# Weights from float64: the lower word's shift made by ScalarE as a scaled, rounded integer

## The chip, the cores and the metric

One NeuronCore of a Trainium2 chip runs the whole program. The metric is device time in microseconds (us) from start to end of one execution. Beside its tensor engine (TensorE; PE and, for weight loads, PEld in the profile) the core has VectorE (DVE), ScalarE (ACT), GpSimd (POOL) and SyncE (SP), which here issues all DMA transfers.

## What is computed

A chunked state-space scan ("attention") on x (4 x 8 x 768 x 32), followed by two dense expert layers on the 3072 tokens with 256 features:

```python
y = scan(x, a, B, C)                  # chunks of 32 tokens, state 16 x 32 per head
x = y as (3072, 256)
h = x @ moe_w_in;  g = maximum(0.01 * h, h);  x = g @ moe_w_out      # 256 -> 2048 -> 256
h = maximum(x @ moe2_w_in, 0);  out = (h * h) @ moe2_w_out           # 256 -> 2048 -> 256
```

The inputs of the scan are float32; the four weight matrices (524,288 numbers each) are float64 and enter the core as pairs of 32-bit words.

## The kernel before

**Scan.** 12 pieces (4 batches, 3 pieces of 256 tokens each). `scan_piece` is a generator of 24 small steps: scale factors (`mx`, `sc`), the decay scans `lt` and `e1`, fp16 halves of the operands, block-diagonal copies (`kbd`, `xbh`, `xbl`, `sbd`), three sets of small matmuls (`S`, then `Y` twice), the state scan `stt`, and at the end `yh` (line 334, ScalarE) and `yl` (line 335, VectorE), one pair for each of the two feature halves: the input of the experts as a rounded part and a rest.

**Experts.** Every product is made of three matmuls (high x low, high x high, low x high). `Phase.hmm` (lines 363 to 365) makes 512 columns of the hidden layer, `act` takes them from PSUM on ScalarE and splits them into `gh` and `gl` (line 379, VectorE; in layer 2 also the square of line 377), `omm` (lines 391 to 396) makes the output. `ORDER` names the phases (layer, block of pieces); `due` says how many scan steps are to be done at which place.

**Weights.** The four matrices are cut into 8 pieces each, `[128, 2, 256]` 64-bit words, 512 KB. A piece goes through four functions, and one call of `w_step` moves four pieces on by one function each:

- `load_w` (line 118): the transfer into the tile `wst`;
- `split_w` (line 127, ScalarE): the upper words `w1`, taken as f32, are scaled by 2^-112;
- `split_w1` (VectorE): line 133 shifts the lower words `w0` right by 29 bits, so that the three bits stay that end an f32 mantissa; line 134 puts in the upper word shifted left by 3, line 135 the sign: `w0` is the f32 value;
- `split_w2`: line 146 (ScalarE) rounds it to the matmul's format, line 147 (VectorE) makes the rest.

`w0` and `w1` are every second word of the tile, a stride of 8 bytes. Eight calls of `w_step` follow the first piece of the scan, others are called between the groups of the experts' first phases.

**Order.** When the program is built, a scheduler orders the instructions of each engine by what is ready; an engine then runs its queue in that order, each instruction behind its waits. So a change of one operation's engine can change the order of everything around it.

Of the kernel before, what the change touches and what calls it, by code (L numbers as in the profile page):

```python
# [10 lines left out]
F16 = mybir.dt.float16  # L11
I32 = mybir.dt.int32
I64 = mybir.dt.int64
AF = mybir.ActivationFunctionType
ALU = mybir.AluOpType
AX = mybir.AxisListType
# [26 lines left out]
def ssd_moe_kernel(ctx: ExitStack, tc: tile.TileContext, in1, in2, w1i, w1o, w2i, w2o, out):  # L43
# [6 lines left out]
    nc = tc.nc  # L50
# [17 lines left out]
    lr = cp.tile([4, P], F32, name="lr")  # L68
    nc.scalar.activation(lr, ones, AF.Lrelu)
    delta = cp.tile([P, U, T], F16, name="delta")  # L70
# [37 lines left out]
    def load_w():  # L108
        nm, c = wq.pop(0)
        if nm == "2o" and c >= 5:  # L110
            st = yp.tile([P, 2, 256], I64, tag="y2", name="wst")
        else:
            st = wp.tile([P, 2, 256], I64, tag="w", name="wst")
        if nm[1] == "i":
# [6 lines left out]
    def split_w():  # L121
        nm, c, sl, st = w_loaded.pop(0)
        v = st.bitcast(I32).rearrange("p k (f two) -> p k f two", two=2)
        w0, w1 = v[:, :, :, 0], v[:, :, :, 1]


        nc.scalar.activation(w1.bitcast(F32), w1.bitcast(F32), AF.Copy, scale=2.0**-112)
        w_half.append((nm, c, sl, w0, w1))

    def split_w1():  # L130

        nm, c, sl, w0, w1 = w_half.pop(0)
        nc.vector.tensor_single_scalar(w0, w0, 29, ALU.logical_shift_right)  # L133
        nc.vector.scalar_tensor_tensor(w0, w1, 3, w0, ALU.logical_shift_left, ALU.bitwise_or)  # L134
        nc.vector.scalar_tensor_tensor(w0, w1, -(1 << 31), w0, ALU.bitwise_and, ALU.bitwise_or)  # L135
        w_full.append((nm, c, sl, w0.bitcast(F32)))

    def split_w2():
# [5 lines left out]
        else:  # L144
            h, l = w_hi[nm][sl], w_lo[nm][sl]
        nc.scalar.activation(h, w, AF.Copy)
        nc.vector.tensor_tensor(l, w, h.bitcast(F32), ALU.subtract)  # L147

    def w_step():
        if w_full:  # L150
            split_w2()
        if w_half:
            split_w1()
        if w_loaded:
            split_w()
        if wq:
            load_w()
# [15 lines left out]
    def scan_piece(p, tiles, get_y):  # L173
# [59 lines left out]
        ch = sp.tile([P, U, T], F16, tag="f2", name="ch")  # L233
        nc.scalar.activation(him, bt_t, AF.Copy, scale=sbp)
        nc.scalar.activation(ch, ct_t, AF.Copy, scale=scc)
        yield
# [16 lines left out]
        xh = sp.tile([P, U, D], F16, tag="xh", name="xh")  # L253
        nc.scalar.activation(xh, x_t, AF.Copy, scale=sx)
        yield
# [298 lines left out]
```

## Time and profile before

| | |
|---|---|
| time, median of 3 runs (lowest to highest) | 662.59 us (661.88 to 662.81) |
| the profiled execution: its time; its span | 663.11 us; 661.3 us |
| busy: PE, DVE, ACT | 605.9, 466.9, 400.6 us |
| mean granted TensorE clock | 0.984 of full speed |
| chain that ended last | PE 72%, DVE 19%, ACT 5% |

The span goes from the first to the last instruction; the execution's time is 1.8 us longer. An engine's busy time is the time in which it ran anything. A mean duration of one instruction includes its latency; two that follow each other without a wait overlap, so their common time is less than the sum. In the strips of 40 slices a digit is the busy share in tenths.

### The profile page before, as it was taken

To read this page: it belongs to the slowest core of one execution; us is meant where nothing else is said; L and a number is where in the kernel's file an instruction comes from. 1 tells how busy PE (TensorE), PEld (TensorE's weight loads), DVE (VectorE), ACT (ScalarE), POOL (GpSimd) and SP (SyncE) were. 2 spreads that over 40 slices of the span, in tenths; PEclk is the share of its full clock that TensorE was granted. 3 is DMA by queue.
4 is the path that set the end of the run, shared out by engine and by line. 5 is a ranking of instruction groups with operands and counts; after the bars stand their busy time and mean duration, and the time that the engine had idled before them with its cause. 6 is when DMAs were issued, how large, how long until landed. Compare 5 with 4: busy or idle time off the path is not lost.

```text
span 661.3 us, 11324 instructions
## 1 busy us (share of the span) xinstructions
PE 605.9 (92%) x4464; PEld 521.1 (79%) x4464; DVE 466.9 (71%) x1016; ACT 400.6 (61%) x714; POOL 5.2 (1%) x14
## 2 busy tenths in 40 slices
PE   0286679998989999999999999999999999999997
PEld 0285679998889888899988788778788878788886
DVE  7989998999998884398594497583596422554543
ACT  4877686866678584395484485475575443444442
POOL 3000000000000000000000000000000000000000
PEclk9997789999999999999999999999999999999999
DMA  8663434110122020010020020030000000000000
GB/s 324 237 186 123 149 96 129 41 65 10 41 73 73 1 89 1 1 64 26 1 88 1 0 73 1 1 104 0 1 1 1 1 32 2 0 1 0 33 1 32
DMA packets 12469, 34.80 MB, mean 53 GB/s; under 512 B 1152, under 2 KB 2176, under 8 KB 12416
## 3 DMA queue, kind: packets, MB, share of 16 engines
q1 hardware_dynamic: 12416, 34.08, 15.8%
q8 instruction: 35, 0.57, 0.4%
q14 instruction: 18, 0.15, 0.1%
HBM read 30.93 MB, written 3.15 MB: 52 GB/s over the span
## 4 chain that ended last, share of the span: by engine, by line
PE 72%; DVE 19%; ACT 5%; issue 2%; DMA 2%; SPq 0%; DVEq 0%; ACTq 0%
PE o L391 12%; PE hp L363 11%; PE hp L364 11%; PE o L392 11%; PE hp L365 11%; PE o L396 11%; DVE gl L379 3%; DVE wst L135 2%; DVE wst L134 2%; DMA wst<-w1i 1%; DVE wst L133 1%; DMA wst<-w2i 1%; DVE e L260 1%; DVE lt L244 1%; DVE w2o L147 1%
## 5 line engine op out<-in xcount | busy, mean ns | idle before, releaser
L379 DVE TENSOR_TENSOR gl<-t,gh 128x512 fp32r<-128x512 f32 x192 | 132.0, 688 | 124.8 <-ACT t L374 81.8
L373 ACT ACTIVATE gh<-hp 128x512 fp32r<-128x512 f32 x96 | 57.3, 597 | 85.8 <-PE o L392 69.4
L378 ACT CAST gh<-t 128x512 fp32r<-128x512 f32 x96 | 59.5, 620 | 59.8 <-DVE t L377 47.1
L391 PE MATMUL o<-gh,wl1o 128*128 128x256 f32 (+1 forms) x256 | 89.0, 361 | 3.4 <-DVE wl1o L147 3.4
L363 PE MATMUL hp<-yl,wh1i 128*128 128x256 f32 (+1 forms) x256 | 88.9, 348 | 3.1 <-DVE yl L335 1.7
L364 PE MATMUL hp<-yh,wh1i 128*128 128x256 f32 (+1 forms) x256 | 88.8, 347 | 0.0
L365 PE MATMUL hp<-yh,wl1i 128*128 128x256 f32 (+1 forms) x256 | 88.1, 344 | 0.0
L377 DVE TENSOR_TENSOR t<-t 128x512 f32<-128x512 f32 x96 | 66.1, 689 | 30.3 <-ACT t L376 29.9
L391 PE MATMUL o<-gh,w2o 128*128 128x256 f32 (+1 forms) x256 | 84.3, 345 | 3.3 <-DVE yl L404 1.4
L363 PE MATMUL hp<-yl,wh2i 128*128 128x256 f32 (+1 forms) x256 | 86.8, 339 | 0.0
L365 PE MATMUL hp<-yh,wl2i 128*128 128x256 f32 (+1 forms) x256 | 86.6, 338 | 0.0
L364 PE MATMUL hp<-yh,wh2i 128*128 128x256 f32 (+1 forms) x256 | 86.3, 337 | 0.0
L392 PE MATMUL o<-gh,wh1o 128*128 128x256 f32 (+1 forms) x256 | 85.6, 348 | 0.0
L376 ACT ACTIVATE t<-hp 128x512 f32<-128x512 f32 x96 | 57.4, 598 | 45.8 <-PE hp L365 44.0
L392 PE MATMUL o<-gh,w2o 128*128 128x256 f32 (+1 forms) x256 | 82.0, 336 | 0.0
L396 PE MATMUL o<-gl,wh1o 128*128 128x256 f32 (+1 forms) x256 | 63.4, 349 | 0.9 <-DVE gl L379 0.9
L396 PE MATMUL o<-gl,w2o 128*128 128x256 f32 (+1 forms) x256 | 61.6, 339 | 0.0
L391 PEld LDWEIGHTS o<-gh,wl1o 128*128 128x128 f32 x256 | 50.4, 197 | 12.3 <-DVE wl1o L147 4.0
L363 PEld LDWEIGHTS hp<-yl,wh1i 128*128 128x128 f32 x256 | 50.0, 196 | 9.4 <-DVE yl L335 2.1
L374 ACT ACTIVATE t<-hp 128x512 f32<-128x512 f32 x96 | 56.9, 593 | 0.0
L391 PEld LDWEIGHTS o<-gh,w2o 128*128 128x128 f32 x256 | 48.1, 188 | 10.9 <-DVE yl L404 2.1
L364 PEld LDWEIGHTS hp<-yh,wh1i 128*128 128x128 f32 x256 | 50.1, 196 | 6.3 <-issue 0.9
(148 smaller groups left out, 1101.9 us busy)
## 6 DMA issues: line engine op xcount, KB each, us to landing
in<-in SPq DMA_DIRECT2D x12, 640.0 KB, 3.9
in<-in SPq DMA_DIRECT2D x12, 512.0 KB, 3.5
wst<-w1i SPq DMA_DIRECT2D x8, 512.0 KB, 8.6
wst<-w1o SPq DMA_DIRECT2D x8, 512.0 KB, 4.0
wst<-w2o SPq DMA_DIRECT2D x8, 512.0 KB, 3.5
wst<-w2i SPq DMA_DIRECT2D x8, 512.0 KB, 4.0
out_t<-ob SPq DMA_DIRECT2D x8, 256.0 KB, 2.3
out_t<-ob SPq DMA_DIRECT2D x8, 128.0 KB, 2.5
```

The lines of the kernel that those rows point to most:

```text
L363: nc.tensor.matmul(hp, wh, self.xl[:, k, :n], start=(k == 0), stop=False)
L364: nc.tensor.matmul(hp, wh, self.xh[:, k, :n], start=False, stop=False)
L365: nc.tensor.matmul(hp, wl, self.xh[:, k, :n], start=False, stop=(k == KI - 1))
L373: nc.scalar.activation(gh, hp, AF.Lrelu)
L374: nc.scalar.activation(t, hp, AF.Lrelu)
L376: nc.scalar.activation(t, hp, AF.Relu)
L377: nc.vector.tensor_tensor(t, t, t, ALU.mult)
L378: nc.scalar.copy(gh, t)
L379: nc.vector.tensor_tensor(gl, t, gh.bitcast(F32), ALU.subtract)
L391: nc.tensor.matmul(self.o[d], wl, gh, start=(m == 0), stop=False)
L392: nc.tensor.matmul(self.o[d], wh, gh, start=False, stop=False)
L396: nc.tensor.matmul(self.o[d], wh, gl, start=False, stop=(m == KO - 1))
```

## The change

The shift of line 133 is taken out of `split_w1`. In its place `split_w` issues a second ScalarE instruction: it reads `w0` as an unsigned 32-bit integer, multiplies it by a little less than 2^-29, adds a little less than -0.5, and writes the result rounded to an integer, which is the word's upper three bits.

```diff
     def split_w():
         ...
         nc.scalar.activation(w1.bitcast(F32), w1.bitcast(F32), AF.Copy, scale=2.0**-112)
+
+
+        nc.scalar.activation(
+            w0, w0.bitcast(U32), AF.Copy, scale=2.0**-29 * (1 - 2.0**-14), bias=7.5 * 2.0**-14 - 0.5
+        )
         w_half.append((nm, c, sl, w0, w1))

     def split_w1():

         nm, c, sl, w0, w1 = w_half.pop(0)
-        nc.vector.tensor_single_scalar(w0, w0, 29, ALU.logical_shift_right)
         nc.vector.scalar_tensor_tensor(w0, w1, 3, w0, ALU.logical_shift_left, ALU.bitwise_or)
         nc.vector.scalar_tensor_tensor(w0, w1, -(1 << 31), w0, ALU.bitwise_and, ALU.bitwise_or)
```

In the changed file line 127 becomes 128, the new instruction is line 131, lines 134 and 135 become 139 and 140, and every later line is 5 higher (146, 147, 334 and 335 become 151, 152, 339 and 340).

The order changes on all engines until about the fourth piece of the scan. Three places:

VectorE, first piece of the scan, where the scale factors `sc` are made between the first two weight pieces. Before:

```order
L135 SCALAR_TENSOR_TENSOR wst<-wst 128x512
L195 TENSOR_SCALAR dg<-ident,m_134 3x3
L133 TENSOR_SCALAR wst<-wst 128x512
L203 TENSOR_SCALAR eb<-S 128x3
L134 SCALAR_TENSOR_TENSOR wst<-wst 128x512
L204 TENSOR_SCALAR eb<-eb 128x3
L147 TENSOR_TENSOR wl1i<-wst,wh1i 128x2x256
L205 TENSOR_SCALAR sc<-eb 128x3
L206 TENSOR_SCALAR isc<-eb 128x3
L244 SCALAR_TENSOR_TENSOR lt<-in_117,delta 128x512
```

And after:

```order
L140 SCALAR_TENSOR_TENSOR wst<-wst 128x512
L200 TENSOR_SCALAR dg<-ident,m_134 3x3
L139 SCALAR_TENSOR_TENSOR wst<-wst 128x512
L208 TENSOR_SCALAR eb<-S 128x3
L152 TENSOR_TENSOR wl1i<-wst,wh1i 128x2x256
L209 TENSOR_SCALAR eb<-eb 128x3
L249 SCALAR_TENSOR_TENSOR lt<-in_117,delta 128x512
L210 TENSOR_SCALAR sc<-eb 128x3
```

The scan `lt` now stands ahead of `sc`; it stood behind it.

ScalarE, first piece, from the copy of the state's input (`d1s`) to the first `yh`. Before:

```order
L306 ACTIVATE d1s<-Y,kk 128x32x8
L314 CAST shl<-stt 128x16x16
L127 ACTIVATE wst<-wst 128x512
L146 ACTIVATE wh1i<-wst 128x2x256 x2
L127 ACTIVATE wst<-wst 128x512
L180 COPY sbd<-t_305 32x16x32 x2
L127 ACTIVATE wst<-wst 128x512
L334 ACTIVATE yh<-Y,fac 128x256
```

And after:

```order
L311 ACTIVATE d1s<-Y,kk 128x32x8
L128 ACTIVATE wst<-wst 128x512
L131 ACTIVATE wst<-wst 128x512
L319 CAST shl<-stt 128x16x16
L151 ACTIVATE wh1i<-wst 128x2x256 x2
L128 ACTIVATE wst<-wst 128x512
L131 ACTIVATE wst<-wst 128x512
L185 COPY sbd<-t_305 32x16x32 x2
L128 ACTIVATE wst<-wst 128x512
L131 ACTIVATE wst<-wst 128x512
L128 ACTIVATE wst<-wst 128x512
L339 ACTIVATE yh<-Y,fac 128x256
```

Two splits stand between `d1s` and `shl`, where there was none, and three instead of one between `sbd` and `yh`.

ScalarE, second piece of the scan, ahead of its `kbd` copies. Before:

```order
L146 ACTIVATE wh1o<-wst 128x512
L374 ACTIVATE t<-hp 128x512
L127 ACTIVATE wst<-wst 128x512 x2
L373 ACTIVATE gh<-hp 128x512
L235 ACTIVATE ch<-in_298,sc 128x512
L234 ACTIVATE him<-in_299,sbp 128x512
L254 ACTIVATE xh<-in_298,sc 128x512
```

And after:

```order
L379 ACTIVATE t<-hp 128x512
L128 ACTIVATE wst<-wst 128x512
L131 ACTIVATE wst<-wst 128x512
L128 ACTIVATE wst<-wst 128x512
L151 ACTIVATE wh1o<-wst 128x512
L240 ACTIVATE ch<-in_298,sc 128x512
L239 ACTIVATE him<-in_299,sbp 128x512
L259 ACTIVATE xh<-in_298,sc 128x512
L378 ACTIVATE gh<-hp 128x512
```

Three splits stand there instead of two, and an expert group's `gh` has moved behind the scan's three operations.

## Rows read from the trace of the kernel before

**Rows 1.** The page: busy time of the engines, and their share in 40 slices.

```profile
PE 605.9 (92%) x4464; PEld 521.1 (79%) x4464; DVE 466.9 (71%) x1016; ACT 400.6 (61%) x714; POOL 5.2 (1%) x14
...
PE   0286679998989999999999999999999999999997
...
DVE  7989998999998884398594497583596422554543
ACT  4877686866678584395484485475575443444442
...
PEclk9997789999999999999999999999999999999999
```

**Rows 2.** Busy time of each engine by stage (us from the span's start).

```profile
core 0: us, PE busy (x) PEld busy (x) DVE busy (x) ACT busy (x) POOL busy (x), PEclk, DMA share, GB/s
...
8.00:33.80 25.80, 4.85 (x114) 4.48 (x114) 24.73 (x62) 20.96 (x36) 0.00 (x0) 1.00 0.80 286
33.80:79.10 45.30, 33.19 (x288) 30.59 (x289) 42.43 (x97) 32.82 (x59) 0.00 (x0) 0.87 0.47 149
79.10:115.40 36.30, 32.47 (x325) 31.33 (x324) 33.23 (x82) 26.39 (x48) 0.00 (x0) 0.88 0.38 119
115.40:168.30 52.90, 49.59 (x484) 47.44 (x484) 52.27 (x115) 38.19 (x69) 0.00 (x0) 1.00 0.14 44
168.30:270.00 101.70, 97.93 (x911) 87.69 (x912) 80.64 (x199) 68.91 (x127) 0.00 (x0) 1.00 0.13 42
270.00:661.30 391.30, 387.31 (x2347) 319.48 (x2345) 229.25 (x458) 211.73 (x375) 0.00 (x0) 1.00 0.06 20
```

**Rows 3.** Groups by line and shape: busy us, mean ns | idle before.

```profile
L133 DVE TENSOR_SCALAR wst<-wst 128x512 int32<-128x512 int32 x32 | 13.2, 420 | 1.2 <-DMA wst<-w1i 1.1
...
L180 ACT COPY xbh<-xh 32x512 f16<-32x512 f16 x48 | 29.4, 613 | 0.6
L127 ACT ACTIVATE wst<-wst 128x512 f32<-128x512 f32 x32 | 21.7, 686 | 11.9 <-DMA wst<-w1i 6.4 <-DMA wst<-w2i 4.3 <-DMA wst<-w1o 0.6
...
L254 ACT ACTIVATE xh<-in,sc 128x512 f16<-128x512 f32 x12 | 8.6, 716 | 0.0
```

**Rows 4.** Timeline, pairs back to back: start us, us of both, engine, line.

```profile
23.56 1.26 ACT L127 ACTIVATE wst<-wst 128x512 f32<-128x512 f32 x2
...
30.80 0.76 DVE L133 TENSOR_SCALAR wst<-wst 128x512 int32<-128x512 int32 x2
31.48 1.29 DVE L134 SCALAR_TENSOR_TENSOR wst<-wst 128x512 int32<-128x512 int32 x2
```

**Rows 5.** VectorE's waits from 8 to 170 us: total us, times, longest.

```profile
DVE wl1i L147 <- ACT wh1i L146: 2.1, 2, 1.8
DVE mkl L292 <- ACT mkh L283: 1.6, 1, 1.6
```

**Rows 6.** Timeline of TensorE: matmuls after its largest gaps [idle before <-releaser].

```profile
33.81 0.58 PE L363 MATMUL hp<-yl,wh1i 128*128 128x256 f32 x1 [1.71 <-DVE yl L335]
...
58.16 0.21 PE L275 MATMUL S<-ch,kbd 128*128 128x32 f16 x1 [4.28 <-ACT kbd L180]
...
73.51 0.39 PE L391 MATMUL o<-gh,wl1o 128*128 128x256 f32 x1 [2.92 <-DVE wl1o L147]
...
95.43 0.18 PE L275 MATMUL S<-ch,kbd 128*128 128x32 f16 x1 [3.41 <-DVE kbd L180]
```

**Rows 7.** Timeline of VectorE: first `yl` of pieces two, three and four.

```profile
79.07 0.48 DVE L335 SCALAR_TENSOR_TENSOR yl<-Y,fac,yh 128x256 fp32r<-128x256 f32 x1
...
115.38 0.47 DVE L335 SCALAR_TENSOR_TENSOR yl<-Y,fac,yh 128x256 fp32r<-128x256 f32 x1
...
168.32 0.48 DVE L335 SCALAR_TENSOR_TENSOR yl<-Y,fac,yh 128x256 fp32r<-128x256 f32 x1
```

**Rows 8.** Timeline of ScalarE in stage A: two of its waits.

```profile
12.63 0.72 ACT L235 ACTIVATE ch<-in,sc 128x512 f16<-128x512 f32 x1 [1.11 <-DVE sc L205]
...
32.15 0.47 ACT L334 ACTIVATE yh<-Y,fac 128x256 fp32r<-128x256 f32 x1 [0.42 <-PE Y L327]
```

More of the change, by code (lines that the diff above doesn't have):

```diff
@@ L13 @@
 I64 = mybir.dt.int64
+U32 = mybir.dt.uint32
 AF = mybir.ActivationFunctionType
```

## The prediction

> **What bounds the kernel now.** I read the page first, then the table by stages, then the waits, then the order of the two engines that the change touches. On the page TensorE is busy for 92% of the span, so over the whole program it sets the time [rows 1]. But its slices are low at the left edge and uneven up to about a quarter of the span, while VectorE shows 9 in eight of its first eleven slices. The average hides two regimes, so I cut the span where each of the first four scan pieces hands its `yl` to TensorE: the first matmul of the experts comes at 33.81 us [rows 6], and the next three pieces' first `yl` subtractions start at 79.07, 115.38 and 168.32 us [rows 7].
>
> The table by these stages [rows 2] shows: from 8 us to the first expert matmul (stage A) VectorE is busy 24.73 of 25.8 us; in stage B (33.8 to 79.1) 42.43 of 45.3; in C (to 115.4) 33.23 of 36.3; in D (to 168.3) 52.27 of 52.9. After that it falls to 80.64 of 101.7 and then to 229.25 of 391.3. ScalarE is busy 20.96, 32.82, 26.39 and 38.19 us in A to D: loaded, but not full. TensorE's idle time is 45.3 - 33.19 = 12.1 us in B, 3.8 in C, 3.3 in D, 3.8 in the next 102 us and 4.0 in all of the rest. VectorE itself waits little before 170 us; its longest waits there add up to 2.1 and 1.6 us, both for ScalarE [rows 5]. So until about 168 us VectorE is the engine that hands out the work; then TensorE is full, and nothing on the other engines matters.
>
> Can VectorE's relief reach the end? Only where TensorE waits. Its four large gaps [rows 6] are 1.71 us at 33.81 (for `yl`, VectorE), 4.28 us at 58.16 (for `kbd`, ScalarE), 2.92 us at 73.51 (for `wl1o`, VectorE) and 3.41 us at 95.43 (for `kbd`, VectorE). What can be won at most is the idle time of B, C and D, 19.2 us, plus what a faster start gives. All 32 shifts stand ahead of the fourth piece's `yl`; later nothing changes but the moment at which the rest begins.
>
> **What one operation costs.** The removed shift takes 420 ns, 32 times [rows 3]; back to back two take 0.76 us, so one more costs VectorE 0.34 us [rows 4]. 32 x 0.34 = 10.9 us leave VectorE. The two operations that stay on VectorE cost 0.60 us each back to back (1.29 us for two) [rows 4]. The added ACTIVATE has no row of its own. Its nearest is line 127, the same engine, the same tile with the same 8-byte stride, 128x512 words in and out: 686 ns, or 0.57 us back to back (1.26 us for two) [rows 3, 4]. A copy from fp16 to fp16 takes 613 ns and one from f32 to fp16 with a scale read from a tile 716 ns [rows 3], so word types and a scalar operand move it by a tenth. I take 0.57 us (ends 0.54 and 0.64): 32 x 0.57 = 18.2 us more on ScalarE. So each word moved costs more than it frees: 0.57 against 0.34.
>
> The Trainium skill has a rule against this (ScalarE: Activation LUTs, Rules for kernel authors): multiplies and adds belong on VectorE, which is faster per element. The rows agree on the price, 420 against 686 ns; by the engine time alone the sum would be 18.2 - 10.9 = 7.3 us longer, 669.9 us.
>
> **What moves.** The instructions of each engine are not laid down in program order, and the two printed orders differ in all of A to D, not by one swap per weight piece. I count what stands ahead of each piece's first `yl` on VectorE and first `yh` on ScalarE.
>
> Stage A. VectorE loses 6 shifts (2.0 us), but the new order puts one more line-134, two more line-135 and one more line-147 operation ahead of the first `yl` (2.4 us): net +0.4. ScalarE gets nine more splits and one more rounding, less one line 127: +9 x 0.57 = 5.1 us ahead of the first `yh`, and it has 25.8 - 20.96 = 4.8 us free. In the two places shown, `sc` now stands behind the scan `lt` (so `ch`, which already waits 1.11 us for `sc` [rows 8], starts about 1.1 us later), and two more splits stand ahead of `yh` (1.1 us against a wait of 0.42 us there [rows 8]: about 0.7 more). The ends are 0 and +5.1; I take **+1.3**, a little under 1.8, since some slack lies between.
>
> Stage B. On VectorE ten shifts go and two line-135 operations have already been done in A: -10 x 0.34 - 2 x 0.60 = -4.6 us. ScalarE gets 11 more: +6.3, which makes 39.1 of 45.3 us against VectorE's 37.8. The two engines hand work to each other all the time, and now neither has much air. Ends 0 and -4.6; I take about half, **-2.2**.
>
> Stage C. Five shifts go (-1.7), two weight operations are already done (-1.2), and two reductions of the next piece come ahead of the mark (+1.2 at the same 0.60): -1.7 us. ScalarE +10 x 0.57 = 5.7: 32.1 of 36.3, VectorE 31.5. Ends 0 and -1.7; I take **-1.2**, more than half, as the two engines are even and TensorE's largest gap here waits for VectorE [rows 6].
>
> Stage D. Eleven shifts go (-3.7); the two reductions were done in C, and one `wl`, two `gl` and one square fall behind the mark (six operations, -3.6): -7.3 us. ScalarE gets almost nothing here (two splits, one rounding less and one relu less). But TensorE is idle only 3.3 us, and part of that is its wait for other things. Ends 0 and -3.3; I take **-1.5**.
>
> SyncE's queue gets a few loads in a different place, among them one weight load ahead of the second piece's second input, which is needed only in stage B; the waits of line 127 for its data are hidden as soon as ScalarE is later than before, so I cost both at nothing. GpSimd's order is unchanged. After D TensorE's order is the same in both kernels except for a few rows.
>
> Sum: +1.3 - 2.2 - 1.2 - 1.5 = -3.6 us. The profiled execution took 663.11 us, so 659.5; the median of the runs, 662.59, is 0.5 lower, so **659.0 us**.
>
> **Rivals.** *ScalarE takes over as the bound (slower).* Its queue is in order, and the scan's copies (`kbd`, `mkh`, `d1s`, `shl`, `sbd`, `yh`) now stand behind the added splits. For it: 39.1 us against 37.8 in B, 32.1 against 31.5 in C, and the largest gap of TensorE already waits for ScalarE's `kbd` [rows 6]. Against it: in D ScalarE has 52.9 - 38.19 = 14.7 us of air. It decides as soon as ScalarE's work ahead of a piece's `kbd` or `yh` ends later than VectorE's. Price: the whole +5.1 in A, nothing won in B and C, -1.5 in D: +3.6, 666.2 us. The rule of the skill above points here.
>
> *VectorE's relief comes through whole.* A at 0, B -4.6, C -1.7, D -3.3: -9.6, 653.0 us. On top, the clock: in B and C its mean is 0.87 and 0.88 of full speed, in A and D 1.00 [rows 2]. With two levels, 2.4 and 1.2 GHz, that is 2 x (0.13 x 45.3 + 0.12 x 36.3) = 20.5 us at the lower level, up to 10.2 us of matmul time lost; the three largest gaps lie in these same two stages [rows 6]. If the gaps shrink and a third of this goes, 3.4 us more are won: 649.6 us. For it: VectorE is nearly without waits up to 170 us. Against it: ScalarE's load, and the largest gap waits for ScalarE. The skill (TensorE: Matmul & The Clock Gate, HAM oscillation) describes waits that put the clock back in just this way; the low clock in these stages agrees.
>
> *No change.* The order puts other weight work where the shifts were, as in A, and TensorE's idle time in B to D stays: within 1.3 us of 662.6.
>
> *The edit does not do what it says.* If an integer in and out took the engine two passes, the new operation would cost some 0.57 us more, 6.3 us in B and 5.1 in A on an engine without that air: about +8 on top, 671 us. The even times of fp16 and f32 copies [rows 3] speak against it.
>
> **How the numbers follow.** Forecast 0.45, ScalarE as the bound 0.25, whole relief 0.15, no change 0.12, a dearer operation 0.03. A difference of 0.2%, 1.3 us, is what a measurement of this kernel can tell from none. Faster: 0.45 + 0.15 = 0.60; same 0.12; slower 0.25 + 0.03 = 0.28. The range goes from 651.5, inside the whole relief without the clock, to 666.5, just past ScalarE as the bound; outside lie the clock's part of the one, some of the other and the dear operation. The forecast's own range, with the ends of A to D half used, is 655 to 661.
>
> **What would show it.** Right: the new line on ScalarE at 0.65 to 0.72 us, VectorE's total down by some 13 us, ScalarE's up by 22; the first expert matmul 0.5 to 2 us later than 33.81; the second piece's `yl` earlier than 79.07 by about 1 us, the fourth's earlier than 168.32 by 3 to 6; TensorE's busy time the same, and its idle time in B to D under 16 us. Wrong: the second `yl` later than 80 us with ScalarE above 90% busy in B (the first rival), or a fourth `yl` 8 us earlier with an end that follows it.

## The result and the profile after

The changed kernel takes 653.71 us (median of 4 runs, 653.03 to 654.31) against 662.24 us of the kernel before (660.41 to 662.81): a ratio of 0.9876, 95% interval 0.9852 to 0.9899, so 8.2 us faster by the ratio. The forecast was 659.0 us, 3.6 us faster; nearest to the measured time is the rival "VectorE's relief comes through whole", put at 653.0. Of all executions of this document one, of 1182.74 us in the run e11 below, lies some 500 us outside the rest of its kernel and is in none of the figures.

The profiled execution took 654.30 us with a span of 652.5 us, 8.8 us less than the 661.3 before. The marks and stages of the kernel before come from an execution of 663.11 us, 0.9 above the median, so a difference of single executions may be off by about as much. The page's busy times and granted clock (against [rows 1]):

```profile
PE 601.4 (92%) x4464; PEld 517.9 (79%) x4464; DVE 456.5 (70%) x984; ACT 415.9 (64%) x746; POOL 5.1 (1%) x14
...
PEclk9997889999999999999999999999999999999999
```

VectorE lost 10.4 us and 32 instructions, ScalarE gained 15.3 us and 32. TensorE's busy time fell by 4.5 us with the same 4464 matmuls; its idle time (span less busy time) fell from 55.4 to 51.1 us. So about half of the 8.8 us is idle time of TensorE, and half is time that it no longer took for the same matmuls.

The same stages as in [rows 2], cut at this kernel's own marks (first expert matmul, first `yl` of pieces two to four):

```profile
core 0: us, PE busy (x) PEld busy (x) DVE busy (x) ACT busy (x) POOL busy (x), PEclk, DMA share, GB/s
8.00:35.38 27.38, 4.85 (x114) 4.48 (x114) 24.91 (x58) 25.36 (x45) 0.00 (x0) 1.00 0.82 281
35.38:75.14 39.76, 31.83 (x296) 29.56 (x296) 38.04 (x85) 38.71 (x71) 0.00 (x0) 0.89 0.54 175
75.14:108.91 33.77, 30.76 (x317) 29.55 (x317) 31.33 (x77) 31.23 (x59) 0.00 (x0) 0.93 0.37 115
108.91:155.05 46.14, 43.74 (x447) 42.73 (x447) 45.18 (x98) 34.50 (x65) 0.00 (x0) 1.00 0.12 39
```

In A and B VectorE and ScalarE are both busy for 91 to 97% of the time; in C for 93 and 92%. Two engines that hand each other work were both that full here, which the forecast did not believe. The marks themselves, from the timelines of TensorE and VectorE (against [rows 6] and [rows 7]):

```profile
35.38 0.58 PE L368 MATMUL hp<-yl,wh1i 128*128 128x256 f32 x1 [1.68 <-DVE yl L340]
...
75.14 0.48 DVE L340 SCALAR_TENSOR_TENSOR yl<-Y,fac,yh 128x256 fp32r<-128x256 f32 x1
...
108.91 0.48 DVE L340 SCALAR_TENSOR_TENSOR yl<-Y,fac,yh 128x256 fp32r<-128x256 f32 x1
...
155.05 0.48 DVE L340 SCALAR_TENSOR_TENSOR yl<-Y,fac,yh 128x256 fp32r<-128x256 f32 x1
...
187.24 0.48 DVE L340 SCALAR_TENSOR_TENSOR yl<-Y,fac,yh 128x256 fp32r<-128x256 f32 x1 [1.50 <-ACT yh L339]
```

The fifth piece's `yl` in the kernel before, not shown yet:

```profile
196.52 0.48 DVE L335 SCALAR_TENSOR_TENSOR yl<-Y,fac,yh 128x256 fp32r<-128x256 f32 x1 [0.52 <-ACT yh L334]
```

Beside them, what the prediction counted of VectorE's own work ahead of each mark (its terms for VectorE, added up from the start):

| mark | before, us | after, us | moved | VectorE's count |
|---|---|---|---|---|
| first expert matmul | 33.81 | 35.38 | +1.6 | +0.4 |
| second `yl` | 79.07 | 75.14 | -3.9 | -4.2 |
| third `yl` | 115.38 | 108.91 | -6.5 | -5.9 |
| fourth `yl` | 168.32 | 155.05 | -13.3 | -13.2 |
| fifth `yl` | 196.52 | 187.24 | -9.3 | -10.9 |
| end of the span | 661.3 | 652.5 | -8.8 | -10.9 |

The plain count of VectorE's work gives the `yl` marks of pieces two to four within 0.6 us; it misses the first mark by 1.2 and the fifth by 1.6. (At the fourth, four operations had only fallen behind the mark; by the fifth they are done.) The lead of 9.3 us then loses only 0.5 us to the end.

The groups of the two ScalarE operations of a weight piece, against line 127 in [rows 3]:

```profile
L128 ACT ACTIVATE wst<-wst 128x512 f32<-128x512 f32 x32 | 22.3, 696 | 6.1 <-DMA wst<-w1i 5.9
L131 ACT ACTIVATE wst<-wst 128x512 int32<-128x512 uint32 x32 | 22.2, 695 | 0.0
```

The integer operation costs what the float one does, 695 against 696 ns, as forecast. TensorE's three large gaps in B and C [rows 6], 4.28, 2.92 and 3.41 us, have become (timeline of TensorE):

```profile
54.40 0.19 PE L280 MATMUL S<-ch,kbd 128*128 128x32 f16 x1 [2.81 <-ACT kbd L185]
...
68.47 0.38 PE L396 MATMUL o<-gh,wl1o 128*128 128x256 f32 x1 [1.73 <-DVE wl1o L152]
...
71.63 0.39 PE L396 MATMUL o<-gh,wl1o 128*128 128x256 f32 x1 [1.48 <-DVE wl1o L152]
...
89.16 0.18 PE L280 MATMUL S<-ch,kbd 128*128 128x32 f16 x1 [2.00 <-DVE kbd L185]
```

The two waits for `kbd` became shorter by 1.5 and 1.4 us; the one for `wl1o` was split in two, 1.73 and 1.48 us, and is not shorter in sum.

### The profile page after: what moved, and what is told of

It is laid out like the page before. It is cut to its first block, busy times and chain, and to the rows that moved or that the text cites. A ratio compares the mean times of both kernels' runs of the same rounds, so it can differ in the third digit from the quotient of the medians.

```text
span 652.5 us, 11330 instructions
## 1 busy us (share of the span) xinstructions
PE 601.4 (92%) x4464; PEld 517.9 (79%) x4464; DVE 456.5 (70%) x984; ACT 415.9 (64%) x746; POOL 5.1 (1%) x14
## 4 chain that ended last, share of the span: by engine, by line
PE 73%; DVE 14%; ACT 8%; issue 2%; DMA 2%; SPq 0%; ACTq 0%; DVEq 0%
PE o L396 12%; PE hp L368 12%; PE o L401 11%; PE o L397 11%; PE hp L369 11%; PE hp L370 11%; DVE gl L384 2%; DVE wst L140 2%; DVE wst L139 1%; ACT xbh L185 1%; DMA wst<-w1i 1%; ACT wst L131 1%; DVE lt L249 1%; PE Y L331 1%; ACT wst L128 1%
```

## The experiments

Each ratio is against executions of the kernel before made beside it on the same chip; those had medians of 661.82 us (the first four experiments), 661.12 (the next four) and 661.23 (the last two). The theory was: VectorE's queue decides when the pieces are ready, so its relief comes through to the end. Rival 1: the gain comes from the value being made on ScalarE, or from the new order as such. Rival 2: ScalarE's load takes part of the gain back, as the forecast had it.

**Relief put back (e1).**

```diff
+        nc.vector.tensor_single_scalar(w0, w0, 0, ALU.logical_shift_right)
         nc.vector.scalar_tensor_tensor(w0, w1, 3, w0, ALU.logical_shift_left, ALU.bitwise_or)
```

> The changed kernel with a shift right by 0 put back on VectorE behind the new ScalarE instruction: VectorE has its 32 operations of 0.34 us again, ScalarE keeps its 32 more. Theory (VectorE's queue was what TensorE waited for, and its relief comes through to the end): the whole gain goes, 662 to 667 us against about 662.2 before. Rival 1 (the gain comes from the value being made on ScalarE early, off VectorE's chain, or from the new order as such): 654 to 658 us.

Measured: 662.89 us, ratio 1.0015 (1.0002 to 1.0027). The gain is gone, all of it. Stages B and D of this run, with VectorE as busy as in [rows 2]:

```profile
34.77:79.65 44.88, 32.76 (x292) 30.16 (x293) 43.17 (x98) 41.89 (x76) 0.00 (x0) 0.89 0.50 156
...
114.87:167.67 52.80, 49.48 (x484) 47.32 (x482) 52.05 (x115) 39.26 (x72) 0.00 (x0) 1.00 0.13 43
```

ScalarE makes the value here too, and is busy 41.89 us in B, against 38.71 in the shorter B of the changed kernel; the second `yl` comes at 79.65 us. The first half of rival 1 falls.

**ScalarE's load without the relief (e2).** The kernel before, with

```diff
-        nc.scalar.activation(w1.bitcast(F32), w1.bitcast(F32), AF.Copy, scale=2.0**-112)
+        nc.scalar.activation(w1.bitcast(F32), w1.bitcast(F32), AF.Copy, scale=2.0**-56)
+        nc.scalar.activation(w1.bitcast(F32), w1.bitcast(F32), AF.Copy, scale=2.0**-56)
```

> The kernel before with ScalarE's scaling by 2^-112 made in two steps of 2^-56: 32 more ScalarE instructions of 0.57 us, VectorE as before. Theory: ScalarE's load costs what it cost in the first stage of the changed kernel, 1 to 2 us, and little after, 662.5 to 665 us. Rival 2 (ScalarE's load takes back a good part of the gain): 666 us or more.

Measured: 662.58 us, ratio 1.0011 (0.9997 to 1.0025): 32 more ScalarE instructions beside a full VectorE cost at most 0.25%. The first expert matmul and the second `yl` of this run (TensorE's and VectorE's timelines), and its stages B and C:

```profile
37.17 0.58 PE L364 MATMUL hp<-yl,wh1i 128*128 128x256 f32 x1 [1.94 <-DVE yl L336]
...
79.24 0.48 DVE L336 SCALAR_TENSOR_TENSOR yl<-Y,fac,yh 128x256 fp32r<-128x256 f32 x1
```

```profile
37.17:79.24 42.07, 31.79 (x291) 29.24 (x292) 40.84 (x93) 40.35 (x73) 0.00 (x0) 0.91 0.48 154
79.24:114.75 35.51, 31.46 (x322) 30.30 (x322) 33.22 (x82) 29.30 (x53) 0.00 (x0) 0.91 0.38 122
```

The experts start 3.4 us later than before, and by the second `yl` 0.2 us of that is left. The order had put three more weight operations of VectorE ahead of the first `yl` than before (about 1.5 us), and these no longer stood in B; the rest of the delay was made up there as well, by fewer waits: VectorE was idle for 1.2 us in B (42.07 less 40.84), 2.9 before. So a term for the first start may not be added to one for B: what counts at the second `yl` is the work in VectorE's queue up to there.

**Relief without ScalarE's load (e3).** The kernel before, with the lower word left out (`z0` is a constant zero, read with stride 0):

```diff
-        nc.vector.tensor_single_scalar(w0, w0, 29, ALU.logical_shift_right)
-        nc.vector.scalar_tensor_tensor(w0, w1, 3, w0, ALU.logical_shift_left, ALU.bitwise_or)
+        nc.vector.scalar_tensor_tensor(w0, w1, 3, z0, ALU.logical_shift_left, ALU.bitwise_or)
```

> The kernel before without the shift: the lower word is left out (the three last mantissa bits become 0, by an OR with a constant zero of the same operation), so VectorE loses its 32 operations and ScalarE gets none. Theory: the same relief of VectorE, and the first stage 1.6 us shorter than in the changed kernel: 650 to 653 us. Rival 1: no gain without ScalarE making the value, 660 to 663 us. Rival 2: well below the changed kernel, under 648 us.

Measured: 654.37 us, ratio 0.9889 (0.9868 to 0.9911). That is a little above the expected 650 to 653, and no better than the change. Its first expert matmul and its second and fourth `yl`:

```profile
31.28 0.58 PE L365 MATMUL hp<-yl,wh1i 128*128 128x256 f32 x1 [1.65 <-DVE yl L337]
...
73.47 0.48 DVE L337 SCALAR_TENSOR_TENSOR yl<-Y,fac,yh 128x256 fp32r<-128x256 f32 x1
...
152.88 0.48 DVE L337 SCALAR_TENSOR_TENSOR yl<-Y,fac,yh 128x256 fp32r<-128x256 f32 x1
```

It starts the experts 4.1 us ahead of the changed kernel, is 1.7 us ahead at the second `yl`, 2.2 at the fourth, and 0.8 at the end of the span. Rival 1's "no gain without ScalarE" falls, and so does rival 2: without ScalarE's load there is nothing more to win in the time, though the marks come some 2 us earlier.

**The first eight pieces back on VectorE (e4).**

```diff
+        if nm != "1i":
             nc.scalar.activation(
                 w0, w0.bitcast(U32), AF.Copy, scale=2.0**-29 * (1 - 2.0**-14), bias=7.5 * 2.0**-14 - 0.5
             )
...
+        if not (nm != "1i"):
+            nc.vector.tensor_single_scalar(w0, w0, 29, ALU.logical_shift_right)
```

> The changed kernel, but the eight pieces of the first matrix keep the shift on VectorE; the other 24 have it on ScalarE. Theory: the first stage is again as before (first expert matmul at 33.8 instead of 35.4 us), and the relief is 24 of 32 parts: 652 to 655 us, about the changed kernel's 653.7 or a little below. Rival 1 (the order as such): no better than chance, 654 to 662 us.

Measured: 654.49 us, ratio 0.9894 (0.9862 to 0.9926). The start is back, as expected (timelines of TensorE and, for the fifth `yl`, VectorE):

```profile
33.63 0.58 PE L371 MATMUL hp<-yl,wh1i 128*128 128x256 f32 x1 [1.98 <-DVE yl L343]
...
185.38 0.48 DVE L343 SCALAR_TENSOR_TENSOR yl<-Y,fac,yh 128x256 fp32r<-128x256 f32 x1
```

but the time is that of the changed kernel, or a little above. It does not tell the theory from the order; it shows again that the later start costs nothing that lasts. And VectorE's count does not fit here: 24 shifts are 8.2 us, yet the fifth `yl` comes 11.1 us earlier than before, 1.9 ahead of the changed kernel, which lost all 32. The mean granted clock of this execution was 0.995, against 0.984 in the one profiled before and 0.990 after; of the four executions, two at 0.995 took 653.2 and 653.1 us, two at 0.990 took 655.8 and 656.9.

**The early and the late half alone (e11, e10).** The same two conditions, with `nm[0] == "1"` and `nm[0] == "2"` for the pieces that ScalarE gets.

> The changed kernel with the shift of the last 16 weight pieces (the two matrices of the second layer) left on VectorE: relief in stages A and B alone, 16 x 0.34 = 5.4 us of VectorE. Theory (all VectorE work ahead of a piece's yl counts one for one, and a later start of the first expert matmul is made up in B, since the queue behind it is shorter): second yl at 75 to 75.5 us, and 4 to 5 us won in all, 657 to 658 us. Rival (the sum on record: a later start adds, half of B's relief comes through): about -1 us, 661 us.

> The changed kernel with the shift of the first 16 weight pieces left on VectorE: relief in stages C and D alone, the same 5.4 us, the first expert matmul at 33.8 us. Theory: second yl at 79, fifth yl some 5 us earlier than 196.5, and 4 to 5 us won in all, 657 to 658 us; the two halves add up to the whole. Rival (TensorE's idle time in C and D caps it, as the sum on record had it): -2.7 us, 659.5 us.

Measured: early 657.28 us, ratio 0.9931 (0.9913 to 0.9950), 4.6 us won; late 657.81 us, ratio 0.9943 (0.9929 to 0.9956), 3.8 us won. The two add up to 8.4 us, the whole to 8.2. The rival's numbers for the early half, 661, and for the late one, 659.5, are out of both intervals (655.4 to 657.8 and 656.4 to 658.2). The marks of the early half come from one more execution of the same kernel:

> The kernel with the relief in the first 16 weight pieces alone, once more for its profile. Theory: second yl at 75 to 75.5 us (79.07 before), and the lead then stays about the same to the end, 656 to 658 us. Rival (the sum on record): second yl at 77.5 to 78.5 us.

Its time was 656.94 us. Second and fifth `yl` of that run:

```profile
74.49 0.48 DVE L343 SCALAR_TENSOR_TENSOR yl<-Y,fac,yh 128x256 fp32r<-128x256 f32 x1
...
190.26 0.48 DVE L343 SCALAR_TENSOR_TENSOR yl<-Y,fac,yh 128x256 fp32r<-128x256 f32 x1 [0.52 <-ACT yh L342]
```

The second `yl` is 4.6 us ahead of before although the experts start 1.6 us later; at the fifth the lead is 6.3 us. In the late half the marks, and the stages B to D, are

```profile
77.76 0.48 DVE L343 SCALAR_TENSOR_TENSOR yl<-Y,fac,yh 128x256 fp32r<-128x256 f32 x1
...
191.11 0.48 DVE L343 SCALAR_TENSOR_TENSOR yl<-Y,fac,yh 128x256 fp32r<-128x256 f32 x1 [1.50 <-ACT yh L342]
```

```profile
33.67:77.76 44.09, 32.43 (x289) 29.55 (x290) 42.44 (x97) 36.32 (x66) 0.00 (x0) 0.85 0.47 152
77.76:113.22 35.46, 32.47 (x325) 31.45 (x324) 32.52 (x77) 29.69 (x55) 0.00 (x0) 0.90 0.39 122
113.22:158.73 45.51, 43.73 (x448) 42.73 (x447) 44.94 (x99) 34.53 (x65) 0.00 (x0) 1.00 0.13 40
```

1.3 us ahead at the second `yl`, where nothing was taken away yet and 79 was expected, and 5.4 at the fifth, 4.1 more, from relief in C and D alone. TensorE's idle time in C and D fell by 2.4 us (from 7.14 to 4.77), near the 2.7 that the sum on record had taken for them; its busy time over the whole program fell as well, from 605.9 to 603.8 us, which the sum had not.

**The other order (e6).** The two ScalarE instructions of `split_w` change places.

> The changed kernel with its two ScalarE instructions of a weight piece in the other order: the same work on each engine, and an order of its own. Theory (the load of the queues decides, not the order): within 1.5 us of the changed kernel's 653.7. Rival (the order as such): 3 us or more away from it.

Measured: 654.41 us, ratio 0.9896 (0.9880 to 0.9911): 0.7 us above the changed kernel by the medians, 1.3 by the ratios. The same work in another order gives nearly the same time; a weak test, since the counts ahead of the marks stayed the same. The runs together test the order better. Each has one of its own, and what is won goes with the number of shifts that VectorE no longer makes: none for 0 (e1, e2), 4.6 and 3.8 us for 16 (e11, e10), 7.0 for 24 (e4), 6.9 to 8.2 for 32 (e6, e3 and the change). So the second half of rival 1, the order as such, falls with them.

**More relief (e9).** The changed kernel without the line that puts in the sign.

> The changed kernel without the operation that puts in the sign (so the weights are all positive): VectorE loses 32 x 0.60 = 19.2 us more, ScalarE nothing. Theory if VectorE is still the bound up to the fourth yl: 8 to 15 us more, 639 to 646 us. Rival (after the change TensorE or ScalarE is the bound in B to D): less than 4 us more, 650 to 653 us.

Measured: 649.20 us, ratio 0.9814 (0.9801 to 0.9828), 4.1 us less than the changed kernel by the two ratios, for 19.2 us less on VectorE: at the edge of the rival, which had less than 4, and half of the least that the theory had. After the change VectorE is no longer the bound by itself. Stages B and D:

```profile
33.89:70.78 36.89, 31.36 (x296) 29.54 (x296) 33.19 (x77) 33.37 (x62) 0.00 (x0) 0.91 0.58 196
...
101.95:149.07 47.12, 44.47 (x443) 43.79 (x443) 41.93 (x92) 43.84 (x82) 0.00 (x0) 0.96 0.15 49
```

In D no engine is full here: TensorE is busy for 94%, ScalarE for 93% and VectorE for 89%. The changed kernel lies where VectorE's relief begins to lose its worth.

**Two tries at a faster version (e8, e12).** In e8 GpSimd makes the weights' rest:

```diff
-        nc.vector.tensor_tensor(l, w, h.bitcast(F32), ALU.subtract)
+        nc.gpsimd.tensor_tensor(l, w, h.bitcast(F32), ALU.subtract)
```

> The changed kernel with the weights' rest (line 152) subtracted on GpSimd, idle after the first 6 us, instead of VectorE: 32 x 0.60 = 19.2 us less on VectorE, as in the run without the sign, but with the whole result. Theory (VectorE's load decides, and GpSimd does not disturb it): about that run's gain over the changed kernel, 648 to 651 us. Rival (GpSimd is slow at it or holds VectorE up, and TensorE waits for the rest of a weight piece): 654 us or more.

Measured: 670.24 us, ratio 1.0132 (1.0110 to 1.0153): slower, as the rival had it. Groups by line; VectorE's two took 683 and 682 ns in the changed kernel:

```profile
L140 DVE SCALAR_TENSOR_TENSOR wst<-wst 128x512 int32<-128x512 int32 x32 | 27.0, 846 | 0.1
L139 DVE SCALAR_TENSOR_TENSOR wst<-wst 128x512 int32<-128x512 int32 x32 | 23.8, 747 | 4.3 <-ACT wst L131 4.2
...
L152 POOL TENSOR_TENSOR wl1o<-wst,wh1o 128x512 fp32r<-128x512 f32 x8 | 14.7, 1839 | 26.4 <-ACT wh1o L151 17.7 <-DVE gl L384 8.7
```

GpSimd takes up to 1.84 us for one in the mean of a group, and VectorE's operations beside it become up to a quarter longer in the mean. That mean hides two cases: 22 of the 32 operations of line 140 do not overlap one of GpSimd's and take 0.68 us, the ten that do take 1.22 us on average. The one that starts at 72.02 us takes 1.80, beside one of GpSimd's from 71.95 to 73.27. In e12 one more of the four copies of `kbd` and of `sbd` goes from ScalarE to VectorE (`"vvaa"` becomes `"vvva"`):

> The changed kernel with one of the two ScalarE copies of each of kbd and sbd moved to VectorE: per scan piece 2 x 0.28 us more on VectorE and 2 x 0.61 less on ScalarE, whose copies TensorE's largest gaps wait for. Theory (VectorE's load decides): +0.28 x 8 = 2 us on VectorE up to the fourth piece, 0 to 2 us slower than 653.7. Rival (after the change ScalarE's copies are the bound): 1 to 3 us faster, 651 to 653 us.

Measured: 655.32 us, ratio 0.9915 (0.9894 to 0.9936), not clearly apart from the changed kernel and not faster: no sign that ScalarE's copies are the bound after the change. None of the versions with the whole result beats the changed kernel.

## Why the prediction was wrong in size

**Right:** what bounds the kernel. VectorE's queue sets the pace up to the fourth piece (e1, e3), and in the changed kernel its counts ahead of the marks of pieces two to four gave the measured marks; in e4 they did not. The price of the new instruction (0.57 us back to back), the first expert matmul about 1.3 us later (measured 1.57, by the two places shown: `ch` at 13.78 instead of 12.63 us, `yh` at 34.34 instead of 32.15), TensorE's idle time in B to D under 16 us (13.3), the sign of the whole. One of its own signs of being wrong came, a fourth `yl` 8 us earlier with an end that follows it (13.3 and 8.8). And the four gaps that it reads as TensorE's large ones are those from the first expert matmul on: in A TensorE waits longer, 5.93 us for `sbd` from ScalarE at 31.09 us alone (6.29 after the change). Nothing in the sum hangs on that.

**The step that failed: the halving of B, and TensorE's busy time, put at no change.** The prediction had -4.6, -1.7 and -7.3 us of VectorE work, and took -2.2, -1.2 and -1.5 of them, because only TensorE's idle time could be won. By the two profiled executions (a stage's length less TensorE's busy time in it), in us:

| TensorE | forecast | measured |
|---|---|---|
| idle, A | +1.3 | +1.6 |
| idle, B | -2.2 | -4.2 |
| idle, C | -1.2 | -0.8 |
| idle, D | -1.5 | -0.9 |
| idle, whole span | -3.6 | -4.3 |
| busy, whole span | 0 | -4.5 |
| span | -3.6 | -8.8 |

The idle time came out nearly as forecast: B won twice its term, C and D a little less than theirs. What the sum lacked is the busy time, expected to stay the same. All of its 4.5 us lie ahead of the fourth `yl`: there TensorE was busy for 106.3 us in B to D instead of 115.3, 8.9 less, and of these 4.4 came back behind the mark, with the 37 matmuls that had moved there. Part of it is the clock (below); what the rest is stays open. The table tells where the time went, not why: in e2 TensorE was busy for 603.6 us, 2.3 less than before, and the span stayed the same. That VectorE's relief is the cause is shown by e1, where the gain goes with it. On VectorE the marks moved, stage by stage: B -5.5 (from +1.6 to -3.9), C -2.6, D -6.8. Three reasons were given for taking less than VectorE's work, and the runs speak to each:

- *ScalarE, now as loaded as VectorE, would take half of B's gain back.* It took nothing that shows in the time: its load alone cost at most 0.25% (e2), and the relief without its load won no more than the change (e3).
- *TensorE's idle time caps D at 3.3 us.* D's idle time fell by 0.9 us only, so the cap was not reached, and yet the fourth `yl` came 6.8 us earlier against the third. A mark on VectorE is not a mark on TensorE: in D TensorE ran 484 matmuls before and 447 after ahead of the fourth `yl`, and the rest moved behind it. The mistake was to take idle time for all that can be won.
- *The later start of +1.3 us adds to the sum.* It came, and it was made up in B (e2, e4, e11). Of the 1.6 us, 0.4 is weight work that is missing from VectorE's queue afterwards; for the rest VectorE waited, 2.5 us in A where it had been 1.1, and waited less in B, 1.7 us instead of 2.9.

The 10.9 us of VectorE work gave 8.2 us (early 4.6, late 3.8). What is missing goes after the fourth `yl`, where TensorE is nearly full: between the fourth and the fifth `yl` the lead falls by 4.0 us, where the four operations that had fallen behind the mark are 2.4, and to the end by 0.5 more.

**The clock** was left out of the forecast; the rival of the whole relief had it as an extra on top of its 653.0. By the stages' mean clock, B and C held 2 x (0.13 x 45.3 + 0.12 x 36.3) = 20.5 us at the lower of the two levels before, and 2 x (0.11 x 39.76 + 0.07 x 33.77) = 13.5 us after. Its price can be read from executions of one and the same kernel, whose clock and span are listed run by run: over 73 executions of the first eight experiments' kernels and of the kernel before beside them, a microsecond more at the lower level (2 x (1 - mean clock) x span, as a deviation from the mean of its own kernel) goes with 0.23 us more of span, with a correlation of 0.75. By that price 7.0 us less at the lower level are worth about 1.6 of the 8.2 us. That is a correlation; by the four executions of e4 (3.2 us longer with 6.5 more at the lower level) the price is 0.5, which gives some 3.5. Two runs bear on the cause. In e10 B and C hold 2 x (0.15 x 44.09 + 0.10 x 35.46) = 20.3 us at the lower level, as before, and 3.8 us are won. In e2, with ScalarE's load and no relief, they hold 2 x (0.09 x 42.07 + 0.09 x 35.51) = 14.0 us, nearly as after, and nothing is won. So the relief wins without the clock, and the gain is not the clock's alone; how much of the 8.2 us the clock adds, 1.6 or 3.5, stays open.

**The rivals.** That "VectorE's relief comes through whole" gave 653.0 us, 0.7 from the measured 653.7, is in part luck: its -9.6 is idle time, with A at 0 and D at -3.3, where +1.6 and -0.9 came, and the busy time that made up for it is not in it. "ScalarE as the bound", held at 0.25, was wrong: with both engines above 90% in B and C the time still followed VectorE (e1). The rule of the Trainium skill on which it leaned (ScalarE: Activation LUTs, Rules for kernel authors: multiplies and adds belong on VectorE) is right about the price of one operation, 420 ns for the shift against 695 for the scaling that replaced it, and wrong as a guide to the time of this kernel, where VectorE was the full engine.

## What to carry to other kernels

Where one engine is full over a stretch and nearly without waits, count its work ahead of each point at which it hands something on: that count, before and after, is the first forecast. Here it needed no discount for another engine that became as full; it was within 0.6 us at three marks of the changed kernel, and 3 us off at the fifth `yl` of e4. Do not add what a change costs at the first hand-over to what it wins at the second, as long as it is the same queue. And do not take the idle time of the engine that is fed for all that can be won: its busy time for the same work can fall too, here by as much as its idle time. Moving an operation from a full engine to one with room paid here although the operation became dearer, up to the point at which the next relief (here 19.2 us for 4.1) shows that the others are full too.

## What the runs showed of the hardware that was not expected

ScalarE reads unsigned 32-bit integers and writes rounded 32-bit integers with a stride of 8 bytes at the price of f32: 695 against 696 ns for 128x512. VectorE and ScalarE, which hand each other the weight pieces, were busy for 93 and 92% of a stage of 34 us (C). GpSimd's subtraction of 128x512 words took 1.48 to 1.84 us in the means of its groups (e8), and VectorE's operations on the weight tiles grew from 683 to 747 and from 682 to 846 ns in the mean beside it: those of line 140 that overlap a subtraction took 1.22 us, the others 0.68.
